# One core, hashed attention and two MLPs: hash matmuls in column halves, copies moved between engines, and a first head without on-chip DMAs

## The chip, the cores and the metric

The kernel runs on one core of a Trainium2 chip. The metric is the device time of one execution in microseconds (us). The kernel before takes 844.27 us (median of three runs, 843.8 to 844.47).

## The reference

Attention with a mask from a locality-sensitive hash, over 2 batches x 8 heads, 768 positions, 64 features a head, followed by two MLPs over all 1536 tokens (512 features, 2048 hidden), everything in float32:

```
q_bits = (q @ proj > 0); k_bits = (k @ proj > 0)        # proj: 64 x 6
mask   = bucket(q_bits) == bucket(k_bits)               # bucket: the 6 bits as a number
scores = where(mask, q @ k.T / 8, -1e9)
attn   = softmax(scores);  x = attn @ v                 # per head, then heads side by side
x = softplus(x @ w_in) @ w_out                          # first MLP
out = (h * clip(h + 3, 0, 6) / 6) @ w2_out, h = x @ w2_in
```

The weights of the MLPs arrive as 64-bit floats and are converted on the chip with integer operations.

## The kernel before, in words

**Precision.** Products run in a fast float32 form of TensorE (fp32r) on a high and a low part: `qa` holds the scaled q's high part in partitions 64 to 127 and its low part in 0 to 63, `ka` holds k's high part twice, `kb` k's low part in its first 64 partitions. The score of a tile is a matmul of `qa` with `ka` plus one of `qb` with `kb` (L392, L393); `qb` holds the high part of q, and the 32 rows from 64 on in `qb` and `kb` carry the hash bits, so that a pair of equal buckets gets a score apart from all others.

**A head.** `prepare(h)` loads k and q into one tile `raw` (k in partitions 0 to 63, q in 64 to 127), k twice into `rawk`, and v into `vx`. It makes the parts (L313 to L331), copies q's high part into `qb` by a DMA, and hashes: two float32 matmuls with 128 output columns (L340) accumulate the dots of both sequence halves in one PSUM tile `dots` of 128 rows (32 rows each for q and k of either half), one VectorE operation compares them (L356), and four DMAs bring the bits to the rows of `qb` and `kb` where they belong (L365). `attend(h)` goes through six tiles of 128 queries. Each has four score matmuls, the row maximum on VectorE (L406), a small bias operation (L413), the exponential on ScalarE (L421), six transposes on TensorE into one PSUM tile (L432), and a copy of these to SBUF (`even`; L226 is the copy helper on ScalarE, L228 on VectorE). When all six are there, the value matmuls run (L448), two at once, as each has 64 output columns and its own half of the PSUM rows. Then `xa` copies the result, three transposes turn it back (L470), `rec` is the reciprocal of the row sums (L474, L478) and `norm` multiplies by it (L485). For each pair of heads the normed result is transposed again (L512) and cut into high and low part: the first MLP's input.

**The MLPs.** For each of 2 layers, 3 groups of 512 tokens and 16 pieces of 128 hidden features: 12 hidden matmuls (L605), an activation chain over ScalarE, VectorE and (first layer only) one GpSimd subtraction (L231), and 12 matmuls into four accumulators (L697, L699). The weights are converted piece by piece (L552 to L576). Twelve of the first layer's 32 pieces are converted during the attention, the rest when SBUF comes free behind it, and the second layer's when the first layer's have been used.

**The order of the work.** All operations go into a `Schedule`: each with a cost per engine that may do it (A ScalarE, D VectorE, P GpSimd, T TensorE, S SyncE for DMA issues), what it reads and writes, and a due time (`prio`, from `TH`, `WHEN`, `STEP`, `PROJECT`, `ACTIVATE`, `AHEAD`). `run()` simulates the engines when the kernel is built: it takes, of the operations that can start soonest on an engine, the one with the lowest due time, and emits it. So each engine's order is fixed at build time by these numbers, and where an operation has costs for two engines, the simulation chooses the engine. On the chip each engine works its list in order and waits by semaphores. Score tiles have two PSUM buffers (`two0`, `two1`), transposes one (`two2`), `av` one, and hash, `pt` and `xt` share one (`pre`).

Of the kernel before, what the change touches and what calls it, by code (L numbers as in the profile page):

```python
# [34 lines left out]
TH = 11.573  # L35
WHEN = dict(load_p=-28.21, load_k=-19.20, load_q=-23.34, load_v=-10.79, high_k=-6.00, high_q=-5.57, low_k=-0.24, low_q=-7.00, copy_q=-8.00, dots=-16.00, bits=-14.00, send=-7.00, scores=-3.50, max=-5.62, exp=2.50, turn=0.70, even=4.80, values=17.62, back=16.00, rec=14.00, norm=21.73, x=21.98, x_high=18.00, x_low=15.78)
# [3 lines left out]
SAME = dict(A=0.13, D=0.13, P=0.1, T=0.0, S=0.0, H=0.0)  # L40
ISSUE, LATENCY, DONE = 0.625, 0.65, 0.74
LANES = 8
TICK, WARM = 3.413, 0.374
STEP = 5.682
PROJECT = 8.694
ACTIVATE = -18.000
FETCH = -52.296
AHEAD = 25.891


def f32(ap):
    return ap.bitcast(F32)
# [11 lines left out]
class Operation:  # L64
    def __init__(self, cost, emit, new, touched, prio, dma, duty):
        self.duty = duty
        self.cost, self.emit, self.new, self.touched, self.prio = cost, emit, new, touched, prio
        self.dma = dma
        self.deps, self.next, self.open = [], [], 0
        self.engine = self.done = None  # L70


class Schedule:
# [8 lines left out]
    def add(self, cost, emit, reads=(), writes=(), prio=0.0, after=(), uses=(), dma=0.0, duty=1.0):  # L82
# [3 lines left out]
        op = Operation(cost, emit, list(writes), {*reads, *writes, *uses}, prio, dma, duty)  # L86
# [11 lines left out]
    def run(self):  # L98
        free = dict(A=1.96, D=0.1, P=0.6, T=0.1, S=0.65, H=0.0, G=0.0, M=0.0)
        lanes, busy = [0.0] * LANES, {}  # L100
        ready = {op: self.times(op) for op in self.ops if not op.open}
        while ready:
            options = []
            for op, times in ready.items():
                slot = self.slots(op)
                if slot is not None:
                    for e, t in times.items():
                        at, end, unit = max(free[e], slot, t), op.cost[e], e
                        if e == "T" and busy.get(int(at / TICK) - 1, 0.0) < WARM * TICK:
                            end *= 2  # L110
# [12 lines left out]
            if e == "T":  # L123
                tick = int(start / TICK)
                busy[tick] = busy.get(tick, 0.0) + op.cost[e] * op.duty
# [46 lines left out]
def lsh_attention_two_mlps(  # L172
# [88 lines left out]
    for s0 in (0, D):  # L261
        plan.add(
            dict(S=0.625), lambda e, s0=s0: nc.sync.dma_start(out=p32.ap[s0 : s0 + D, :], in_=proj),
            writes=[p32], prio=WHEN["load_p"], dma=0.06,
        )
    hashes = buffer("heads", [P, 6 * ROWS], F32, "hash", 1, "hash")

    def set_hashes(e):
        nc.vector.memset(hashes.ap, 0.0)
        for i, sign in enumerate((1.0, -1.0)):  # L270
            for rows, c, s in ((slice(0, D), 3 * ROWS + NB * i, -sign), (slice(D, P), 2 * ROWS + NB * i, sign)):
                nc.vector.tensor_scalar(hashes.ap[rows, c : c + NB], p32.ap[rows, :], s, None, op0=ALU.mult)

    plan.add(dict(D=0.7), set_hashes, reads=[p32], writes=[hashes], prio=-20)
# [4 lines left out]
    def prepare(h):  # L279
# [4 lines left out]
        rawk = buffer("heads", [P, S], F32, "rawk", 2, f"rawk{h}")  # L284
        for d, n in ((qa, "qa"), (qb, "qb"), (ka, "ka"), (kb, "kb")):
# [12 lines left out]
        plan.add(  # L298
            first, lambda e: engines[e].dma_start(out=rawk.ap, in_=kv[head][:, :S]),
            writes=[rawk], prio=at + WHEN["load_q"], dma=1.1,  # L300
        )
# [6 lines left out]
        wide, narrow = dict(A=0.74, D=0.48), dict(D=0.88)  # L308

        def scaled(e):  # L310
# [8 lines left out]
            narrow,  # L319
# [5 lines left out]
        plan.add(  # L325
            wide, lambda e: cast(e, ka[h].ap, rawk.ap),
            reads=[rawk], writes=[ka[h]], prio=at + WHEN["high_k"],
        )
# [4 lines left out]
        plan.add(  # L333
            queue, lambda e: engines[e].dma_start(out=f32(qb[h].ap[0:D, :]), in_=f32(qa[h].ap[D:P, :])),
            reads=[qa[h]], writes=[qb[h]], prio=at + WHEN["copy_q"], dma=0.55,
        )
        dots = buffer("ps", [P, 512], F32, "pre", 1, f"d{h}")

        def dot(u):
            nc.tensor.matmul(  # L340
                dots.ap[:, :HALF], hashes.ap[:, (1 - u) * 2 * ROWS : (3 - u) * 2 * ROWS],
                raw.ap[:, u * HALF : (u + 1) * HALF], start=(u == 0), stop=(u == 1),
            )

        last = ()
        for u in range(2):
            last = [
                plan.add(
# [476 lines left out]
```

## Time and profile before

One execution was profiled. It took 844.39 us; the span of its instructions is 842.7 us, the other 1.7 us lie around it.

| | busy us | share of the span | instructions |
|---|---|---|---|
| TensorE matmul (PE) | 799.3 | 95% | 3808 |
| TensorE weight load (PEld) | 604.5 | 72% | 3808 |
| VectorE (DVE) | 558.9 | 66% | 958 |
| ScalarE (ACT) | 451.5 | 54% | 764 |
| GpSimd (POOL) | 92.1 | 11% | 85 |

The granted TensorE clock is full in nearly the whole span (0.999 on average). The load of k twice (`rawk`) moves 384 KB a head, those of k, q, v and the copy of q's high part 192 KB each. The attention takes the first 281 us, the first MLP the time to 573, the second the rest. Matmuls are pipelined and overlap in the records, so a TensorE that is shown busy need not be at its peak; the shares are averages over stages with different limits.

### The profile page before, as it was taken

The numbers are of one execution on the slowest core, as the hardware profiler recorded it, in microseconds if no ns is written. First come the engines' busy times: TensorE is split into PE (matmuls) and PEld (weight loads), VectorE is DVE, ScalarE is ACT, GpSimd is POOL, SyncE is SP. The second block draws the span as 40 slices with busy tenths as digits, with TensorE's granted clock in tenths as the row PEclk, the third lists the DMA queues.
The fourth block names the chain that finished last, engine by engine and source line by source line (L and its number), as shares of the span: only waits on it lengthen the run. The fifth ranks groups of instructions, "written<-read, shape, count | busy, mean of one in ns | idle before, by whom it ended". The sixth has DMA issues, their size and how long they took to land.

```text
span 842.7 us, 10395 instructions
## 1 busy us (share of the span) xinstructions
PE 799.3 (95%) x3808; PEld 604.5 (72%) x3808; DVE 558.9 (66%) x958; ACT 451.5 (54%) x764; POOL 92.1 (11%) x85
## 2 busy tenths in 40 slices
PE   4899999999999999999999999999999999999997
PEld 2666666666666667677888776677888888888886
DVE  4989999999887889964333698989942322232222
ACT  1677677777665767656554766775532322232222
POOL 1000000000000242322222224340000000000000
PEclk9999999999999999999999999999999999999999
DMA  7584323332310650000000255451000100010001
GB/s 191 166 271 103 82 80 93 86 85 75 86 29 28 254 228 0 1 1 1 0 1 1 93 157 167 158 175 50 1 1 1 50 1 1 0 51 1 1 0 51
DMA packets 26771, 59.40 MB, mean 70 GB/s; under 512 B 3680, under 2 KB 7776, under 8 KB 26720
## 3 DMA queue, kind: packets, MB, share of 16 engines
q1 hardware_dynamic: 24224, 52.45, 20.6%
q10 hardware_dynamic: 2496, 6.29, 2.1%
q8 instruction: 30, 0.49, 0.2%
q14 instruction: 21, 0.17, 0.1%
HBM read 49.29 MB, written 3.15 MB: 62 GB/s over the span
## 4 chain that ended last, share of the span: by engine, by line
PE 65%; DVE 16%; ACT 5%; DMA 5%; POOL 4%; issue 4%; SPq 1%; ACTq 0%; DVEq 0%; POOLq 0%
PE ph L605 22%; PE acc L699 16%; PE acc L697 7%; PE av L448 7%; PE tp L432 5%; POOL ml L231 4%; PE sc L392 4%; PE sc L393 3%; DVE gl L231 2%; DVE bits L576 2%; DVE bits L569 2%; PE d L340 2%; ACT e L421 2%; DMA raw<-in_moe_w_out_dram 2%; DVE me L665 2%
## 5 line engine op out<-in xcount | busy, mean ns | idle before, releaser
L605 PE MATMUL ph<-xh,w 128*128 128x512 f32 x768 | 240.8, 395 | 0.8 <-ACT xa L226 0.6
L605 PEld LDWEIGHTS ph<-xh,w 128*128 128x128 f32 x768 | 143.7, 188 | 34.5 <-ACT xa L226 1.3
L605 PE MATMUL ph<-xl,w 128*128 128x512 f32 x384 | 151.2, 394 | 0.0
L421 ACT ACTIVATE e<-sc,bs 128x768 f32<-128x768 f32 x96 | 95.0, 990 | 64.2 <-DVE bs L413 44.9
L634 DVE SCALAR_TENSOR_TENSOR ml<-me,ph 128x512 f32<-128x512 f32 x48 | 33.0, 687 | 124.6 <-ACT me L629 124.6
L697 PE MATMUL acc<-gh,w 128*128 128x512 f32 x384 | 101.0, 400 | 11.7 <-ACT gh L226 11.3
L231 POOL TENSOR_TENSOR ml<-ml,me 128x512 f32<-128x512 f32 x48 | 85.9, 1789 | 210.3 <-DVE me L665 154.2
L406 DVE TENSOR_REDUCE nm<-sc 128x1 f32<-128x768 f32 x96 | 91.7, 955 | 22.1 <-PE sc L393 20.6
L629 ACT ACTIVATE me<-ph,three 128x512 f32<-128x512 f32 x48 | 33.1, 689 | 133.7 <-PE ph L605 130.7
L699 PE MATMUL acc<-w,gh 128*128 128x512 f32 x384 | 97.8, 393 | 0.0
L697 PEld LDWEIGHTS acc<-gh,w 128*128 128x128 f32 x384 | 69.9, 188 | 37.2 <-ACT gh L226 22.7
L605 PEld LDWEIGHTS ph<-xl,w 128*128 128x128 f32 x384 | 72.1, 188 | 17.0
L699 PEld LDWEIGHTS acc<-w,gh 128*128 128x128 f32 x384 | 72.1, 188 | 16.7
L392 PE MATMUL sc<-ka,qa 128*128 128x384 f32 x192 | 76.7, 400 | 7.0 <-ACT e L421 6.6
L432 PE MATMUL tp<-ident,e 128*128 128x128 f32 x576 | 80.1, 275 | 3.2 <-DVE et L228 1.7
L432 PEld LDWEIGHTS tp<-ident,e 128*128 128x128 f32 x576 | 66.8, 140 | 16.0 <-ACT et L226 5.2
L448 PE MATMUL av<-et,vx 128*64 128x384 f32 x384 | 72.1, 498 | 0.0
L393 PE MATMUL sc<-kb,qb 96*128 96x384 f32 x192 | 66.1, 344 | 2.3 <-DMA kb<-bt 2.3
L392 PEld LDWEIGHTS sc<-ka,qa 128*128 128x128 f32 x192 | 36.8, 192 | 38.6 <-ACT e L421 15.5
L676 DVE SCALAR_TENSOR_TENSOR ml<-ph,ml 128x512 f32<-128x512 f32 x48 | 33.0, 687 | 38.7 <-POOL ml L231 38.7
L697 PE MATMUL acc<-gl,w 128*128 128x512 f32 x192 | 54.4, 397 | 2.8 <-ACT xh L226 2.1
L231 DVE TENSOR_TENSOR gl<-ml,gh 128x512 fp32r<-128x512 f32 x48 | 38.5, 801 | 26.0 <-ACT gh L226 26.0
(62 smaller groups left out, 1030.4 us busy)
## 6 DMA issues: line engine op xcount, KB each, us to landing
raw<-in_moe_w_in_dram SPq DMA_DIRECT2D x26, 512.0 KB, 4.6
raw<-in_moe_w_out_dram SPq DMA_DIRECT2D x26, 512.0 KB, 3.5
rawk<-in_kv_dram SPq DMA_DIRECT2D x16, 384.0 KB, 4.2
raw<-in_kv_dram SPq DMA_DIRECT2D x16, 192.0 KB, 3.2
raw<-in_q_dram SPq DMA_DIRECT2D x16, 192.0 KB, 3.4
vx<-in_kv_dram SPq DMA_DIRECT2D x16, 192.0 KB, 2.4
qb<-qa SPq DMA_DIRECT2D x16, 192.0 KB, 4.1
raw<-in_moe_w_in_dram ACTq DMA_DIRECT2D x6, 512.0 KB, 8.8
```

The costliest lines, as they stand in the source:

```text
L231: engines[e].tensor_tensor(out, a, b, op=ALU.subtract)
L392: nc.tensor.matmul(o, qa[h].ap[:, qs], ka[h].ap[:, cs], start=True, stop=False)
L393: nc.tensor.matmul(o, qb[h].ap[0:KB, qs], kb[h].ap[0:KB, cs], start=False, stop=True)
L406: lambda e, sc=sc, t=t: nc.vector.reduce_max(nm.ap[:, t, 0:1], sc.ap[:, :, :HALF], axis=AX.XY, negate=True),
L421: lambda e, sc=sc, ex=ex, t=t: nc.scalar.activation(ex.ap.rearrange("p (u k) -> p u k", u=2), sc.ap[:, :, :HALF], AF.Exp, bias=bs.ap[:, t, ...
L432: nc.tensor.transpose(o, ex.ap[:, c * P : (c + 1) * P], ident.ap)
L448: nc.tensor.matmul(av.ap[u * D : (u + 1) * D, :HALF], vx[h].ap[:, c, :], et[u].ap[:, c, :], start=(c == 0), stop=(c == NT - 1),)
L605: nc.tensor.matmul(bank(), w[:, a, :], x[b].ap[:, kc, :], start=(kc + i == 0), stop=(kc == KC - 1 and i == 2))
L629: dict(A=0.478), lambda e: nc.scalar.activation(e1.ap, bank(), AF.Relu, bias=three.ap),
L634: lambda e: nc.vector.scalar_tensor_tensor(l.ap, e1.ap, 6.0, bank(), op0=ALU.min, op1=ALU.mult),
L697: nc.tensor.matmul(o, w.ap[:, a, cs], b.ap, start=st, stop=sp)
L699: nc.tensor.matmul(o, b.ap[:, cs], w.ap[:, a, :], start=st, stop=sp)
```

## The change

The hash tile `hashes` shrinks from 192 to 64 columns, and its two matmuls write to the two halves of the PSUM rows, each with 64 output columns. They are one operation now. ScalarE alone does the scaling of q, the cast of k and the copy `xa` (except parts of head 0), and of the six `even` copies of a head the tiles 1, 2, 4 and 5; tiles 0 and 3 stay open to VectorE. GpSimd does the subtraction for k's low part (except head 0) and the small sum in `rec`. Head 0 loads no `rawk`, and gets `ka`, the copy of q's high part and the hash bits by compute engines: two half casts, one copy, and four VectorE operations of 32 rows. One of the two loads of `proj` is issued by ScalarE. The planner counts 0.09 where TensorE changes between three kinds of matmul, and all costs and due times get new values.

```diff
-TH = 11.573
+TH = 9.867
-STEP = 5.682
-PROJECT = 8.694
-ACTIVATE = -18.000
-FETCH = -52.296
-AHEAD = 25.891
+SWITCH = 0.09
+STEP = 5.895
+PROJECT = 9.269
+ACTIVATE = -18.456
+FETCH = -54.515
+AHEAD = 31.626
 ...
+                        if e == "T" and op.mode != mode:
+                            end += SWITCH
 ...
-    for s0 in (0, D):
+    for s0, e in ((0, "S"), (D, "A")):
-    hashes = buffer("heads", [P, 6 * ROWS], F32, "hash", 1, "hash")
+    hashes = buffer("heads", [P, 2 * ROWS], F32, "hash", 1, "hash")
 ...
+        if h:
+            rawk = buffer("heads", [P, S], F32, "rawk", 2, f"rawk{h}")
 ...
-        wide, narrow = dict(A=0.74, D=0.48), dict(D=0.88)
+        wide, narrow = dict(A=0.74) if h else dict(A=0.74, D=0.48), dict(P=1.9) if h else dict(D=0.88)
 ...
+            for s0, e in ((0, "D"), (D, "A")):
+                plan.add(
+                    {e: wide[e]}, lambda e, s0=s0: cast(e, ka[h].ap[s0 : s0 + D, :], raw.ap[0:D, :]),
+                    reads=[raw], writes=[ka[h]], prio=at + WHEN["high_k"] - s0,
+                )
 ...
+            plan.add(
+                dict(A=0.74), lambda e: cast(e, qb[h].ap[0:D, :], f32(qa[h].ap[D:P, :])),
+                reads=[qa[h]], writes=[qb[h]], prio=at + WHEN["high_q"],
+            )
 ...
-        def dot(u):
-            nc.tensor.matmul(
-                dots.ap[:, :HALF], hashes.ap[:, (1 - u) * 2 * ROWS : (3 - u) * 2 * ROWS],
-                raw.ap[:, u * HALF : (u + 1) * HALF], start=(u == 0), stop=(u == 1),
-            )
+        def dot(e):
+            for u in range(2):
+                nc.tensor.matmul(
+                    dots.ap[u * D : (u + 1) * D, :HALF], hashes.ap, raw.ap[:, u * HALF : (u + 1) * HALF],
+                    start=True, stop=True,
+                )
+        if h == 0:
+            for u in range(2):
+                for n, x in enumerate((qb, kb)):
+                    rows = slice((2 * u + n) * ROWS, (2 * u + n + 1) * ROWS)
+                    plan.add(
+                        dict(D=0.5),
+                        lambda e, u=u, x=x, rows=rows: nc.vector.tensor_scalar(
+                            x[h].ap[D:KB, u * HALF : (u + 1) * HALF], dots.ap[rows, :HALF], thr.ap[rows, 0:1],
+                            top.ap[rows, 0:1], op0=ALU.is_gt, op1=ALU.mult,
+                        ),
+                        reads=[dots, thr, top], writes=[x[h]], prio=at + WHEN["bits"],
+                    )
+            return
 ...
-                dict(A=0.81, D=0.95), even, reads=[tp], writes=[et[t // n]], prio=step + WHEN["even"],
+                dict(A=0.73) if t % 3 else dict(A=0.73, D=0.88), even, reads=[tp], writes=[et[t // n]], prio=step + WHEN["even"],
 ...
-            dict(A=0.49, D=0.46), lambda e: cast(e, xa.ap, av.ap[:, :HALF]),
+            dict(A=0.44), lambda e: cast(e, xa.ap, av.ap[:, :HALF]),
 ...
-            dict(D=0.08), lambda e: nc.vector.tensor_scalar(rec.ap, den.ap, 1e-9, None, op0=ALU.add),
+            dict(P=0.3), lambda e: nc.gpsimd.tensor_scalar(rec.ap, den.ap, 1e-9, None, op0=ALU.add),
 ...
-            dict(P=1.3), lambda e: minus(e, l.ap, l.ap, e1.ap), reads=[l, e1], writes=[l], prio=prio
+            dict(P=1.8), lambda e: minus(e, l.ap, l.ap, e1.ap), reads=[l, e1], writes=[l], prio=prio
```

## Rows read from the trace of the kernel before

**Rows 1.** Busy time by stretch: stretch, its us, each engine's busy us (instructions), granted clock.
```profile
35.10:260.20 225.10, 217.28 (x1308) 149.30 (x1307) 205.28 (x379) 158.07 (x273) 3.62 (x13) 1.00 0.37 104
281.20:363.80 82.60, 76.69 (x318) 57.56 (x318) 76.02 (x129) 56.89 (x100) 27.88 (x13) 1.00 0.24 90
```

**Rows 2.** Chain of waits, 115 to 132 us: start us, us, engine, tile, line.
```profile
115.67 0.68 PE d L340 x2
...
116.70 0.66 PE tp L432 x6
117.36 0.18 PE sc L392
...
117.71 0.65 PE d L340 x2
...
119.13 1.44 PE av L448 x8
120.57 0.37 PE sc L392
...
122.14 1.44 PE av L448 x8
...
128.15 0.34 PE pt L470 x3
...
129.76 0.96 DVE nm L406
```

**Rows 3.** Groups of instructions, 35.1 to 260.2 us: count, busy us, mean ns, idle before.
```profile
L421 ACT ACTIVATE e<-sc,bs 128x768 f32<-128x768 f32 x85 | 84.2, 990 | 45.8 <-DVE bs L413 39.2 <-DVE qa L320 3.2 <-DVE rec L478 1.6
...
L228 DVE COPY et<-tp 128x768 f32<-128x768 f32 x40 | 37.8, 946 | 0.4 <-PE tp L432 0.4
L226 ACT ACTIVATE et<-tp 128x768 f32<-128x768 f32 x44 | 35.6, 810 | 14.0 <-PE tp L432 13.3
...
L231 DVE TENSOR_TENSOR kb<-raw,ka 64x768 fp32r<-64x768 f32 x13 | 12.2, 942 | 0.0
...
L228 DVE COPY xa<-av 128x384 f32<-128x384 f32 x10 | 5.6, 558 | 2.4 <-PE av L448 2.0
```

**Rows 4.** Instructions in order of time, 0 to 36 us.
```profile
0.80 1.23 SPq L263 DMA_DIRECT2D p<-in_proj_dram  x2
...
2.85 0.16 DVE L272 TENSOR_SCALAR hash<-p 64x6 f32<-64x6 f32 x1 [1.73 <-DMA p<-in_proj_dram]
...
3.21 0.60 SPq L295 DMA_DIRECT2D raw<-in_q_dram  x1
...
7.74 2.90 PE L340 MATMUL d<-raw,hash 128*128 128x384 f32 x4 [7.74 <-DMA raw<-in_q_dram]
...
10.75 0.68 DVE L356 TENSOR_SCALAR bt<-d,thr,top 128x384 fp32r<-128x384 f32 x1 [0.60 <-PE d L340]
...
12.64 0.58 SPq L365 DMA_DIRECT2D kb<-bt  x1
...
17.90 0.66 PE L393 MATMUL sc<-kb,qb 96*128 96x384 f32 x1 [2.33 <-DMA kb<-bt]
```

**Rows 5.** GpSimd's and VectorE's instructions in order of time, in the first MLP.
```profile
309.68 1.62 POOL L231 TENSOR_TENSOR ml<-ml,me 128x512 f32<-128x512 f32 x1 [3.34 <-DVE me L665]
310.06 1.53 DVE L557 TENSOR_SCALAR bits<-bits 128x512 f32<-128x512 f32 x1
311.51 0.75 DVE L562 TENSOR_SCALAR bits<-bits 128x512 int32<-128x512 int32 x2
...
371.64 1.29 POOL L231 TENSOR_TENSOR ml<-ml,me 128x512 f32<-128x512 f32 x1 [3.87 <-DVE me L665]
```

**Rows 6.** Waits: 40 to 260, 281 to 573, 363.8 to 472 us; us, times, longest.
```profile
ACT et L226 <- PE tp L432: 13.3, 17, 1.6
...
DVE ml L676 <- POOL ml L231: 38.7, 29, 1.5
...
DVE ml L676 <- POOL ml L231: 24.9, 17, 1.5
```

More of the change, by code (lines that the diff above doesn't have):

```diff
@@ L64, with __init__ @@
 class Operation:
-    def __init__(self, cost, emit, new, touched, prio, dma, duty):
-        self.duty = duty
+    def __init__(self, cost, emit, new, touched, prio, dma, mode):
+        self.mode = mode
         self.cost, self.emit, self.new, self.touched, self.prio = cost, emit, new, touched, prio
@@ L80, in __init__, with add @@
         self.ops, self.rings = [], {}
-    def add(self, cost, emit, reads=(), writes=(), prio=0.0, after=(), uses=(), dma=0.0, duty=1.0):
+    def add(self, cost, emit, reads=(), writes=(), prio=0.0, after=(), uses=(), dma=0.0, mode="r"):
         deps = list(after)
@@ L85, in add @@
             deps += b.users if b in writes else b.writers
-        op = Operation(cost, emit, list(writes), {*reads, *writes, *uses}, prio, dma, duty)
+        op = Operation(cost, emit, list(writes), {*reads, *writes, *uses}, prio, dma, mode)
         for b in op.touched:
@@ L124, in run @@
                 tick = int(start / TICK)
-                busy[tick] = busy.get(tick, 0.0) + op.cost[e] * op.duty
+                busy[tick] = busy.get(tick, 0.0) + op.cost[e]
+                mode = op.mode
             free[e] = op.done
@@ L324, in prepare @@
         )
[L325 to L328, printed above, removed]
+        if h:
+            plan.add(
+                wide, lambda e: cast(e, ka[h].ap, rawk.ap),
+                reads=[rawk], writes=[ka[h]], prio=at + WHEN["high_k"],
+            )
+        else:
+            for s0, e in ((0, "D"), (D, "A")):
[3 more added lines that the diff above has]
+                )
         plan.add(
@@ L345, in prepare @@
[L345 to L348, printed above, removed]
-                    dict(T=0.66), lambda e, u=u: dot(u),
-                    reads=[raw, hashes], writes=[dots], prio=at + WHEN["dots"], after=last,
-                )
-            ]
+        if h:
+            plan.add(
+                queue, lambda e: engines[e].dma_start(out=f32(qb[h].ap[0:D, :]), in_=f32(qa[h].ap[D:P, :])),
+                reads=[qa[h]], writes=[qb[h]], prio=at + WHEN["copy_q"], dma=0.55,
+            )
+        else:
+            plan.add(
+                dict(A=0.74), lambda e: cast(e, qb[h].ap[0:D, :], f32(qa[h].ap[D:P, :])),
+                reads=[qa[h]], writes=[qb[h]], prio=at + WHEN["high_q"],
+            )
@@ L432, in turn @@
                     nc.tensor.transpose(o, ex.ap[:, c * P : (c + 1) * P], ident.ap)
-            plan.add(dict(T=0.56), turn, reads=[ex, ident], writes=[tp], prio=step + WHEN["turn"])
+            plan.add(dict(T=0.5), turn, mode="t", reads=[ex, ident], writes=[tp], prio=step + WHEN["turn"])
             def even(e, tp=tp, t=t):
```

40 lines of the change are left out of this document (18 added, 22 removed).

## The prediction

> **What bounds the kernel now.** I read the table of stretches first, then the chain of waits, then the groups of instructions, then the first 36 us in order of time. The stretch with 14 of the 16 heads, from the first exponential of head 1 to that of head 15, is 225.1 us long [rows 1], and holds 84 exponentials, six a head, and one more at its edge [rows 3]. So a head takes 225.1 / 14 = 16.08 us. TensorE is busy for 97% of it, VectorE for 91%, ScalarE for 70% (217.28, 205.28 and 158.07 of 225.1), at the upper clock level (2.4 GHz, granted 1.00). Two engines that high leave open which one limits, and a busy TensorE need not be at its peak; the chain answers that. Through the head at 115 us it runs along TensorE instruction behind instruction for some 13 us, and leaves it only at the end of the head, where VectorE's max, copy and subtraction stand in it [rows 2].
>
> TensorE's own need per head can be added up from that chain [rows 2]. A tile with values goes from one av group to the next: 122.14 - 119.13 = 3.01 us, three times: 9.03. A tile without them is six transposes at 0.66 and four score matmuls at 0.18: 1.38, three times: 4.14. The hash is two pieces, 0.68 and 0.65: 1.33. The turn back of the head (pt) is 0.34, and of the x transposes (six per two heads) half of a 0.66 falls to a head: 0.33. Sum 15.2 us. The other 16.08 - 15.2 = 0.9 us is waiting for another engine, mostly at the head's end. So TensorE is the bound, VectorE close behind.
>
> Behind the attention the two MLP layers run at TensorE's pace except where weights are converted: from 281.2 to 363.8 us VectorE is busy for 76.02 of 82.6 us and TensorE issues 318 matmuls [rows 1]; there VectorE limits.
>
> **The change part by part.**
>
> Hash in column halves. Now it is two matmuls with 128 output columns, 1.33 us a head [rows 2]. Afterwards it is two with 64, which can stream together, as the av matmuls do (128x64 against 384 columns). Their eight records take 1.44 us, so four take 0.72. The av group shows two prices beside that: eight records at twice the rate of the hash pieces (0.34 a record) would be 8 x 0.17 = 1.36, so 0.08 is spent at its ends, and the first score matmul behind it takes 0.37 instead of 0.18 [rows 2]. So 0.72 + 0.08 + 0.19 = 0.99, a gain of 0.34; without these prices it is 1.33 / 2 = 0.67. I take 0.45 per head, as the hash may also stand next to an av group and share its switch.
> The Trainium skill, TensorEngine Tiling (Array Packing), section Key Properties, says that a change of tiling mode drains the engine; the 0.37 against 0.18 agrees with it. The section Theoretical Speedup promises up to 2x; by that alone a head would gain 0.67, and the attention 3 us more.
>
> Work taken off VectorE, per head, from [rows 3], divided by 14 heads. The low part of k goes to GpSimd: 0.94. Copies of the transposed tiles: 40 / 14 = 2.86 are on VectorE now, at most 2 (every third of six tiles) may be afterwards: 0.86 x 0.95 = 0.81. The xa copy, 10 of 14: 0.40. The scaled q, the k cast and the small sum for the reciprocal, each now on VectorE in some heads: 0.45 together, an estimate from the same rows by their size. Sum 2.6: VectorE falls from 205.28 / 14 = 14.7 to 12.1 us a head. ScalarE gets these copies at its own price (0.81 for a transposed tile, the others in proportion): 0.70 + 0.35 + 0.3 + 0.1 = 1.5, and rises from 158.07 / 14 = 11.3 to 12.8. Both then stand below TensorE's 15.2 - 0.45 = 14.75. So none of this counts directly; it counts only in the 0.9 us of waits. Least: nothing goes (the wait at the head's end is a chain through several engines, and ScalarE is now late in it). Most: all 0.9. I take 0.55, nearer to all than to none, since VectorE's ops stand in that gap in the chain and VectorE then has 2.6 us more room.
>
> GpSimd's subtraction. No row shows 64x768 there. 128x512 takes 1.29 us undisturbed [rows 5], so 768 columns 1.29 x 1.5 = 1.93 us, in front of which nothing is queued but small fills and, new, the sum for the reciprocal. k is ready most of a head early, so 1.93 instead of 0.94 is hidden. What isn't free: GpSimd and VectorE stood in each other's way in the MLP. Beside a subtraction there a 128x512 tensor_scalar took 1.53 us, where two of its kind together take 0.75, and the subtraction itself 1.62 [rows 5]. Bounds per head: nothing (if only max, bias and copies from PSUM fall beside it), or one hindered op, 1.53 - 0.38 = 1.15, stretched by 1.5 to 1.7 of VectorE's time. VectorE has that room, so I take nothing for TensorE.
>
> Attention together: 0.45 + 0.55 = 1.0 us a head over heads 1 to 15: -15 us. Bounds: 0.67 + 0.9 = 1.57 a head gives -24; nothing gained gives 0; a loss is the last rival.
>
> The first head. Now its first finished scores start at 17.90 us, behind this chain [rows 4]: q is issued at 3.21, behind p twice, rawk (the doubled k) and k, and is seen at 7.74; the hash takes 2.90 (four records at twice the 0.34 of later ones), the bits 0.68 from 10.75, then the DMA of the bits is issued at 12.64 and seen 5.3 us later. Afterwards k and q are SP's first DMAs, from 0.80 on, and no rawk is loaded. A tiny DMA is seen 2.85 - 0.80 = 2.05 us after its issue; q with rawk and k, 768 KB, 4.53. So 192 KB cost (4.53 - 2.05) / 4 = 0.6, and q, issued second, at about 1.4, is there at 1.4 + 2.05 + 2 x 0.6 = 4.7, and p, third on SP and on the ACT queue, by about the same. Then VectorE has the hash weights, four at 0.16; half of the k cast, 0.6 at most (by the bits); two low parts at 0.95; four bit ops of 32 rows at 0.6, as columns and not rows set their time: 5.5 us, to 10.2 [rows 3, 4]. ScalarE's three copies at 0.81 and the hash (half of 2.90) lie beside it. So scores start at 10.2 instead of 17.90: -7.7. Bounds: -5.5 (p late by 2) to -8.5. Three kinds of DMA waits go from head 0; those of head 1 are issued earlier and have the whole of head 0 as cover.
>
> The MLP. Its instructions stay; GpSimd's planned cost (1.3 to 1.8) and the due times change the order. VectorE's wait for GpSimd's subtraction is 38.7 us in 281 to 573, of which 24.9 lie in the stretch where TensorE is full and cost nothing [rows 6]. The other 13.8 are what a better order could win at most; a worse one could cost as much. The same instructions, so I take 0.
>
> Sum against the profiled run, 844.39 us (span 842.7 and 1.7 around it; the median of the runs is 0.12 less): 844.3 - 15 - 7.7 = 821.6, or 822 us.
>
> **The rivals.**
>
> *All waits go, and the MLP's order gets better*: 844.3 - 24 - 7.7 - 7 (half of the 13.8) = 806. For it: VectorE gets 2.6 us of room a head. Against it: six tiles pass through two score buffers and one transpose buffer as before.
>
> *ScalarE takes VectorE's place.* Its copies of transposed tiles waited 13.3 us in 17 waits for the transposes, 0.78 each [rows 6]. With four a head, 3.1 us of wait on 12.8 of work make 15.9 against the 16.08 of now, 0.18 a head. Beside that the first head's gain stays: 844.3 - 7.7 - 15 x 0.18 = 834. Against it: a wait in which the engine has nothing due costs nothing.
>
> *The halves don't run at once*: the hash takes 1.33 + 0.27 of switching instead of 1.33 - 0.45 = 0.88; 16 x 0.72 = 11.5 us are missing: 833. Against it: av shows such pairs together.
>
> *GpSimd gets between VectorE and TensorE*, at the head's end. The sum for the reciprocal now stands on GpSimd behind the subtraction, and behind that the reciprocal, xn and the x transposes. If the subtraction starts just before it, it is 1.93 us late, and TensorE has nothing else to do there; a hindered bias op in front of an exponential would cost the same. At 1.93 a head 822 + 15 x 1.93 = 851. It decides from 22.3 / 15 = 1.5 us a head on. For it: the waits at the head's end are there already [rows 2]. Against it: the subtraction is due long before.
> The Trainium skill, SBUF — State Buffer, section Who interferes with whom, says that a VectorE op with two SBUF inputs and a GpSimd op that reads SBUF exclude each other for a whole instruction; the 1.53 us agree for a neighbouring kind, and no run here shows it yet for the bias op, which by that rule would be hit.
>
> **How the numbers follow.** The forecast, 822, has 0.55; all waits gone 0.18; ScalarE 0.13; halves in turn 0.06; GpSimd 0.06; 0.02 for a change that ends within what can be told from none (0.2%, 1.7 us). The range goes from the second case to past the third and fourth: 806 to 836. Faster: all but the last two and part of the ScalarE case, 0.91; same 0.03; slower 0.06.
>
> **What would show it.** Four hash records a head in about 0.8 us with the first score behind them at 0.37. Finished scores from 10 to 11 us. Head to head 15.1 us, TensorE nearer to 15 of that, VectorE near 12, ScalarE near 13. GpSimd's 64x768 at 1.9 us or more. From the last value matmul to the end 561 us (842.7 - 281.2), as now. Wrong if the heads still take 16 us with another engine in the gaps, or the MLP moves by more than 5 us.

## The result and the profile after

The changed kernel takes 832.48 us (median; 832.43 to 832.95) against 844.03 us of the kernel before, run beside it: a ratio of 0.9866, with a 95% interval of 0.9848 to 0.9883. The forecast was 822 us in a range of 806 to 836. So the sign was right and the time lies in the range, but the gain is 11.6 us where 22 had been forecast.

The table of stretches of the changed kernel, to be read beside [rows 1]: stretch, its us, busy us (instructions) of TensorE's matmuls, its weight loads, VectorE, ScalarE and GpSimd, then the granted clock, the DMA share and GB/s. The first stretch goes from the first exponential of head 1 to that of head 15, the second is heads 2 to 5, the third heads 6 to 14; the others are short stretches that are read further down.

```profile
27.60:246.90 219.30, 211.17 (x1305) 143.48 (x1303) 170.75 (x308) 183.91 (x314) 30.05 (x40) 0.99 0.38 109
46.00:110.40 64.40, 59.60 (x367) 40.41 (x366) 62.97 (x119) 59.45 (x103) 9.30 (x12) 1.00 0.45 127
110.40:246.90 136.50, 134.67 (x844) 91.46 (x842) 92.96 (x164) 110.69 (x189) 17.61 (x25) 1.00 0.28 77
...
22.00:26.00 4.00, 2.95 (x20) 2.35 (x19) 3.78 (x5) 2.82 (x5) 1.92 (x2) 1.00 0.20 47
26.00:30.00 4.00, 3.29 (x12) 3.20 (x13) 2.69 (x6) 2.77 (x6) 0.67 (x1) 0.59 0.82 226
265.00:270.00 5.00, 3.89 (x18) 2.88 (x16) 4.62 (x7) 4.36 (x9) 1.35 (x1) 1.00 0.94 366
270.00:275.00 5.00, 3.70 (x12) 2.82 (x13) 5.00 (x9) 4.49 (x9) 1.77 (x2) 0.75 0.03 11
```

The same view of the kernel before, cut at the same heads (2 to 5, then 6 to 14):

```profile
50.40:114.90 64.50, 61.67 (x371) 41.99 (x370) 59.17 (x109) 45.37 (x78) 0.84 (x4) 1.00 0.42 112
114.90:260.20 145.30, 140.82 (x850) 97.00 (x849) 131.96 (x243) 100.65 (x174) 2.68 (x8) 1.00 0.28 73
```

The reader is to see that the relief of VectorE is real (170.75 instead of 205.28 us in heads 1 to 14) and that the gain is not spread evenly. Heads 6 to 14 went from 145.30 / 9 = 16.14 us to 136.50 / 9 = 15.17 us, and TensorE is now busy in 134.67 of the 136.50. Heads 2 to 5 take 64.40 / 4 = 16.10 us, as before, with TensorE idle for 4.8 us. Heads 1 to 14 together went from 225.10 [rows 1] to 219.30 us, 0.41 us a head. TensorE's idle time in them has not fallen: 225.10 - 217.28 = 7.8 us before, 219.30 - 211.17 = 8.1 us now.

Divided at the starts of the exponentials, the 12.1 us by which the span is shorter (842.7 to 830.6) come from these places. (In this table heads 2 to 5 and 6 to 14 are means per head.)

| us | before | after | change in all |
|---|---|---|---|
| first exponential of head 0 at | 20.49 | 13.15 | -7.3 |
| head 0 | 14.6 | 14.4 | -0.2 |
| head 1 | 15.2 | 18.4 | +3.1 |
| heads 2 to 5, each | 16.13 | 16.12 | 0 |
| heads 6 to 14, each | 16.14 | 15.17 | -8.8 |
| head 15 to the first hidden matmul | 13.3 | 12.2 | -1.1 |
| first hidden matmul to the end | 569.2 | 571.5 | +2.3 |

A single head says little: the cut leaves 87 to 101 of TensorE's matmul records in each of heads 6 to 14 of the changed kernel, and these heads take 14.3 to 16.2 us.

What divides heads 2 to 5 from the later ones is shown by the last integer operation of each early weight conversion. The groups of instructions of the changed kernel, 50 to 115 us (count, busy us, mean ns):

```profile
L603 DVE SCALAR_TENSOR_TENSOR bits<-raw,bits 128x512 int32<-128x512 int32 x11 | 7.4, 674 | 0.0
```

The same of the kernel before, 115 to 180 us:

```profile
L576 DVE SCALAR_TENSOR_TENSOR bits<-raw,bits 128x512 int32<-128x512 int32 x5 | 3.3, 683 | 0.0
```

Before, the twelve pieces were spread over heads 1 to 13, the last one ending at 235.8 us: by this operation three of them stood in heads 2 to 5 and eight in heads 6 to 14. Now the planner puts ten into heads 2 to 5, and the last one reaches into head 6 and ends at 115.6 us. Behind that no head holds a conversion. So the two groups are not the same work before and after: heads 6 to 14 lost seven of their eight pieces, and heads 2 to 5 took on seven. Only heads 1 to 14 together hold the same twelve in both kernels.

The chain of waits of the changed kernel, in a head that holds none (start us, us, engine, tile, line), to be read beside [rows 2]:

```profile
118.68 0.66 PE tp L459 x6
119.34 0.17 PE sc L419
...
120.04 1.44 PE av L475 x8
121.48 0.82 PE tp L459 x6
...
123.03 1.09 ACT e L448 x2
...
125.13 0.71 PE tp L459 x6
125.84 0.80 PE d L361 x4
126.64 0.38 PE sc L419
```

The hash is four records in 0.80 us where it was 0.68 and 0.65, and the first score behind it takes 0.38.

The groups of instructions of the changed kernel, 27.6 to 246.9 us, beside [rows 3]:

```profile
L448 ACT ACTIVATE e<-sc,bs 128x768 f32<-128x768 f32 x84 | 83.2, 990 | 19.5 <-DVE bs L440 13.5 <-DVE rec L505 3.9 <-PE tp L459 1.2
L231 ACT ACTIVATE et<-tp 128x768 f32<-128x768 f32 x70 | 56.6, 808 | 13.8 <-PE tp L459 13.1
L236 POOL TENSOR_TENSOR kb<-raw,ka 64x768 fp32r<-64x768 f32 x13 | 23.7, 1822 | 64.3 <-ACT ka L231 63.7 <-DMA kb<-bt 0.3 <-PE av L475 0.2
...
L233 DVE COPY et<-tp 128x768 f32<-128x768 f32 x14 | 13.3, 948 | 2.2 <-PE tp L459 2.2
```

VectorE makes one copy of transposed tiles a head (14 in 14 heads) where it made 2.86, and GpSimd's subtraction takes 1.82 us.

The first instructions of the changed kernel in order of time (start us, us, engine, line, operation, tiles, shapes, and in brackets the idle time before it and what ended it), beside [rows 4]:

```profile
0.78 0.59 SPq L295 DMA_DIRECT2D raw<-in_kv_dram  x1
...
1.43 0.57 SPq L299 DMA_DIRECT2D raw<-in_q_dram  x1
...
4.79 0.56 DVE L321 TENSOR_SCALAR qa<-raw 64x768 fp32r<-64x768 f32 x1 [0.31 <-DMA raw<-in_q_dram]
...
6.13 1.55 PE L361 MATMUL d<-raw,hash 128*64 128x384 f32 x4 [6.13 <-DVE hash L277]
...
8.08 0.67 DVE L373 TENSOR_SCALAR qb<-d,thr,top 32x384 fp32r<-32x384 f32 x1
...
9.72 0.69 PE L420 MATMUL sc<-kb,qb 96*128 96x384 f32 x1 [1.42 <-ACT qb L231]
...
10.93 0.69 PE L420 MATMUL sc<-kb,qb 96*128 96x384 f32 x1 [0.21 <-DVE kb L373]
```

### The profile page after: what moved, and what is told of

Read it like the earlier page. It is cut to its first block, busy times and chain, and to the rows that moved or that the text cites. A ratio compares the mean times of both kernels' runs of the same rounds, so it can differ in the third digit from the quotient of the medians.

```text
span 830.6 us, 10443 instructions
## 1 busy us (share of the span) xinstructions
PE 793.9 (96%) x3808; PEld 596.3 (72%) x3808; DVE 519.8 (63%) x878; ACT 484.7 (58%) x818; POOL 117.6 (14%) x116
## 4 chain that ended last, share of the span: by engine, by line
PE 69%; DVE 18%; ACT 5%; issue 4%; POOL 2%; DMA 1%; POOLq 0%; SPq 0%; ACTq 0%; DVEq 0%
PE ph L632 22%; PE acc L726 16%; PE acc L724 7%; PE av L475 7%; PE tp L459 6%; PE sc L419 4%; PE sc L420 3%; DVE bits L603 3%; DVE w L236 2%; POOL ml L236 2%; DVE bits L596 2%; DVE gl L236 2%; DVE bits L589 2%; DVE bits L584 1%; DVE nm L433 1%
## 5 line engine op out<-in xcount | busy, mean ns | idle before, releaser
L724 PE MATMUL acc<-gh,w 128*128 128x512 f32 x384 | 103.9, 409 | 9.2 <-ACT gh L231 8.9
L236 POOL TENSOR_TENSOR ml<-ml,me 128x512 f32<-128x512 f32 x48 | 80.4, 1676 | 218.7 <-DVE me L692 142.3
L459 PE MATMUL tp<-ident,e 128*128 128x128 f32 x576 | 82.2, 279 | 1.8 <-ACT et L231 1.0
L231 ACT ACTIVATE et<-tp 128x768 f32<-128x768 f32 x79 | 63.9, 808 | 15.1 <-PE tp L459 14.2
L236 DVE TENSOR_TENSOR gl<-ml,gh 128x512 fp32r<-128x512 f32 x48 | 36.8, 767 | 35.7 <-ACT gh L231 35.7
L679 ACT ACTIVATE me<-ph 128x512 f32<-128x512 f32 x48 | 28.4, 591 | 48.2 <-PE ph L632 48.1
```

Source lines behind the costliest of these rows:

```text
L231: nc.scalar.activation(out, in_, AF.Copy)
L236: engines[e].tensor_tensor(out, a, b, op=ALU.subtract)
L459: nc.tensor.transpose(o, ex.ap[:, c * P : (c + 1) * P], ident.ap)
L724: nc.tensor.matmul(o, w.ap[:, a, cs], b.ap, start=st, stop=sp)
```

## The experiments

Ratios are to the kernel before, run beside each kernel on the same chip; the changed kernel's is 0.9866. Where a difference between two variants is given in us, it is the difference of their ratios times 844. "Order kept" means that every engine's list of instructions is that of the kernel named (the changed one, or the one before), and only what one entry does is another.

**Hash at full width again, order kept.** The hash tile has 192 columns again.

```diff
-    dots.ap[u * D : (u + 1) * D, :HALF], hashes.ap, raw.ap[:, u * HALF : (u + 1) * HALF],
-    start=True, stop=True,
+    dots.ap[:, :HALF], hashes.ap[:, (1 - u) * 2 * ROWS : (3 - u) * 2 * ROWS],
+    raw.ap[:, u * HALF : (u + 1) * HALF], start=(u == 0), stop=(u == 1),
```

> The changed kernel with its order of work kept to the letter, but each head's hash again as two matmuls with 128 output columns that accumulate. In the changed kernel's trace a hash holds TensorE for 0.80 us, in the one before for 1.39 us, so 15 heads lose up to 9 us. First theory (TensorE's own work sets the pace of a head, and the column halves are where the heads' gain comes from): slower than the changed kernel by 5 to 9 us, 837 to 841 us. Rival (the heads gain because VectorE was relieved, and TensorE has room for the longer hash): within 2 us of 832.5. Rival of the forecast (the switch into column halves takes back 0.2 to 0.3 us a head): 836 us or less.

Measured: 837.36 us, ratio 0.9913 (0.99 to 0.9926), 4.0 us more than with halves. Heads 6 to 14 take 15.43 us instead of 15.17, heads 2 to 5 16.36 instead of 16.12. So the halves are worth 0.25 us a head here, about half of the 0.45 of the forecast. (The first exponential starts at 14.2 us instead of 13.1, which is part of the 4.0.)

The table of stretches of this experiment, heads 1 to 14, and its chain of waits at a hash with the same neighbours as the one shown above at 125.84:

```profile
29.50:251.80 222.30, 214.18 (x1303) 148.63 (x1301) 171.41 (x308) 183.56 (x314) 30.07 (x40) 1.00 0.38 107
...
127.65 0.70 PE tp L459 x6
128.35 1.29 PE d L361 x4
129.65 0.17 PE sc L419
```

Heads 1 to 14 take 222.30 us here, 15.88 a head. That is 0.20 less than in the kernel before: so much comes from all the rest of the change. The halves bring the other 0.21 of the 0.41.

**The hash in halves alone, in the kernel before, order kept.** The two matmuls of the change replace those at L340, at the place of the second.

> The kernel before with its order kept, and only the hash in column halves (both matmuls where the second stood). First theory (a head loses what the hash loses on TensorE, 1.39 to 0.80 us, less some switching): faster than the kernel before by 4 to 8 us, 836 to 840 us. Rival (VectorE is the bound of the kernel before, so TensorE's saving vanishes): within 2 us of 844.3.

Measured: 843.73 us, ratio 0.9989 (0.9979 to 0.9998). Heads 2 to 5 take 16.17 us and heads 6 to 14 16.06, against 16.13 and 16.14. The records are as short as in the changed kernel (median 537 ns, two at a time), so the halves run at once here too. The table of stretches, heads 1 to 14:

```profile
35.00:259.40 224.40, 213.76 (x1308) 142.87 (x1307) 205.07 (x379) 158.23 (x272) 3.62 (x13) 1.00 0.36 104
```

TensorE is busy for 3.5 us less than the 217.28 of the kernel before, and idle for 10.6 us instead of 7.8: most of what the hash saves turns into waiting. The gain of 0.9 us in all is all that is left, with VectorE as full as it was.

**The low part of k subtracted by VectorE again, order kept.**

```diff
-    narrow, lambda e: minus(e, kb[h].ap[0:D, :], ...
+    narrow, lambda e: minus("D", kb[h].ap[0:D, :], ...
```

> The changed kernel with the planned order kept, but the subtraction for k's low part is issued on VectorE instead of GpSimd (0.94 us a head of VectorE's time against 1.82 on GpSimd). In the changed kernel's trace 6 of 15 such subtractions shut out a small bias operation, which takes up to 1.82 us instead of 0.15, and 2 shut out a weight conversion: 8.7 us in sum. First theory (GpSimd's subtraction holds up the chain from the maximum to the exponential, and so takes back most of what VectorE's relief gives): faster than the changed kernel by 3 to 7 us, 826 to 830 us. Rival (VectorE's room is worth more than these stops): slower by 3 us or more, 836 us up. Third (neither matters, since TensorE has its work): within 1.5 us of 832.5.

Measured: 833.16 us, ratio 0.9866 (0.9851 to 0.9881): the same as the changed kernel. Heads 6 to 14 take 15.29 us. With the copies gone from VectorE, it does not matter which of the two engines subtracts; heads 2 to 5 take 16.14 us too. Whether it mattered with them was not tried.

**The bias operation with one input at a time.** It is the 128x2 operation with two SBUF inputs that stands in front of each exponential; here it is two operations of 128x1.

```diff
-    lambda e, t=t: nc.vector.scalar_tensor_tensor(
-        bs.ap[:, t, :], nm.ap[:, t, 0:1].to_broadcast([P, 2]), 0.5 * BIG, nm.ap[:, t, :], ...
+    lambda e, t=t: (
+        nc.vector.tensor_scalar(bs.ap[:, t, 1:2], nm.ap[:, t, 0:1], 0.5 * BIG, None, op0=ALU.is_lt),
+        nc.vector.tensor_scalar(bs.ap[:, t, 0:1], nm.ap[:, t, 0:1], 0.5 * BIG, nm.ap[:, t, 0:1], ...),
+    ),
```

> The changed kernel with the planned order kept; the small bias operation of a tile (one VectorE operation with two SBUF inputs) is made of two operations with one SBUF input each. GpSimd keeps the subtraction. If an operation with two SBUF inputs is what GpSimd shuts out, the stops of 0.4 to 1.8 us in front of exponentials go, at the price of 96 more short VectorE operations (about 0.07 to 0.1 us each, in the chain to the exponential). First theory: 2 to 5 us faster than the changed kernel, 827 to 830 us, and no bias operation above 0.3 us in the trace. Rival (the stop comes with any operation that reads SBUF, or the price of the second operation eats the gain): 832 us or more.

VectorE and GpSimd of the changed kernel, in order of time, around one subtraction:

```profile
167.00 1.82 DVE L440 SCALAR_TENSOR_TENSOR bs<-nm 128x2 f32<-128x2 f32 x1
168.85 0.95 DVE L326 SCALAR_TENSOR_TENSOR qa<-raw,qa 64x768 fp32r<-64x768 f32 x1
...
166.97 1.83 POOL L236 TENSOR_TENSOR kb<-raw,ka 64x768 fp32r<-64x768 f32 x1 [12.59 <-ACT ka L231]
```

The same place of this experiment:

```profile
168.36 0.15 DVE L441 TENSOR_SCALAR bs<-nm 128x1 f32<-128x1 f32 x1
168.44 0.20 DVE L442 TENSOR_SCALAR bs<-nm 128x1 f32<-128x1 f32 x1
169.22 1.88 DVE L326 SCALAR_TENSOR_TENSOR qa<-raw,qa 64x768 fp32r<-64x768 f32 x1 [0.58 <-ACT qa L319]
...
168.45 1.82 POOL L236 TENSOR_TENSOR kb<-raw,ka 64x768 fp32r<-64x768 f32 x1 [12.69 <-ACT ka L231]
```

In the changed kernel the bias operation starts with the subtraction and is held until it ends: 1.82 us, where it takes 0.15 undisturbed. In the experiment it passes, and the next operation with two SBUF inputs is held instead (1.88 us, where it takes 0.95). Measured: 832.65 us, ratio 0.9856 (0.9841 to 0.9871): not told apart from the changed kernel. So GpSimd does shut VectorE out, 6 of the 96 bias operations are hit (0.41 to 1.82 us), and it costs nothing that can be measured. Heads 2 to 5 take 16.18 us.

**Head 0 with its DMAs, as the other heads.** The order is planned anew.

```diff
-        if h:
+        if True:      # rawk, ka from rawk, qb's high part by DMA
-        if h == 0:
+        if False:     # the four bit operations
```

> The changed kernel with head 0 made as in the kernel before: k loaded twice, high part of q and hash bits moved by DMAs. The order is planned anew. First theory (a later start of head 0 is passed on in full): slower by 6 to 8 us, 838 to 841 us, finished scores near 17 us instead of 9.7. Rival (the early heads wait for their loads and weight conversions anyway, so a late start is made up): within 2 us of 832.5.

Measured: 840.93 us, ratio 0.9952 (0.994 to 0.9965), 7.3 us more than the changed kernel. The first exponential starts at 20.2 us instead of 13.1. So the first head is most of the whole gain.

**VectorE may take all copies again.**

```diff
-    dict(A=0.73) if t % 3 else dict(A=0.73, D=0.88), even, ...
+    dict(A=0.73, D=0.88), even, ...
-    dict(A=0.44), lambda e: cast(e, xa.ap, av.ap[:, :HALF]),
+    dict(A=0.44, D=0.46), lambda e: cast(e, xa.ap, av.ap[:, :HALF]),
-    wide, narrow = dict(A=0.74) if h else dict(A=0.74, D=0.48), ...
+    wide, narrow = dict(A=0.74, D=0.48), ...
```

> The changed kernel, in which VectorE may again take all copies that it might take before: every transposed tile, the scaled q, the cast of k, xa. GpSimd keeps its subtraction; the order is planned anew. First theory (copies matter only where VectorE is the bound, which is heads 1 to 5): slower by 1 to 4 us, 833.5 to 836.5 us. Rival of the forecast (the copies' move gives half of the waits, 0.55 us a head): slower by 8 us, 840 us. Third (they matter nowhere): within 1 us of 832.5.

The table of stretches of this experiment, heads 1 to 14:

```profile
27.30:259.70 232.40, 214.38 (x1305) 143.38 (x1304) 218.45 (x371) 143.53 (x251) 29.91 (x40) 0.99 0.35 102
```

and its groups of instructions in that stretch:

```profile
L233 DVE COPY et<-tp 128x768 f32<-128x768 f32 x63 | 59.9, 950 | 8.3 <-PE tp L459 8.2
...
L231 ACT ACTIVATE et<-tp 128x768 f32<-128x768 f32 x21 | 17.0, 809 | 6.7 <-PE tp L459 6.4
```

Measured: 846.56 us, ratio 1.0016 (1.0001 to 1.003): the gain is gone. Left free, and with the new due times, the planner gives VectorE 63 of 84 copies (40 before the change), and VectorE is busy for 94% of a stretch that is 13 us longer. The heads 6 to 14 take 16.33 us. I had expected the freedom to cost little; that theory fell, and no theory on record went as far.

**The new numbers alone, in the kernel before.** `TH`, `WHEN`, `STEP`, `PROJECT`, `ACTIVATE`, `FETCH` and `AHEAD` are the changed kernel's, and nothing else.

> The kernel before with nothing changed but the due times (TH, WHEN, STEP, PROJECT, ACTIVATE, FETCH, AHEAD), which are those of the changed kernel; costs, engines and instructions stay. First theory (the new due times fit the new split of work only, and by themselves change little): within 3 us of 844.3. Rival (the new due times are themselves what shortens the heads): 838 us or less. Third (they cost by themselves, and the structure's parts make up for it): 847 us or more.

Measured: 854.05 us, ratio 1.0102 (1.0087 to 1.0116). VectorE makes 58 of 84 copies of transposed tiles, heads 2 to 5 take 17.22 us, and first hidden matmul to end 576.7 us (the early conversions reach into that part here, so it doesn't price the MLP's due times by itself). The new numbers are worth nothing alone. What the new structure takes with the old numbers was not tried.

**The early conversions spread again.** In the first form the load of early piece n waits for head n's last exponential.

```diff
-    convert_all(0, range(EARLY), [first_exp])
+    for n in range(4 * EARLY):
+        j, i = divmod(n, 4)
+        prio = time_of(0, 0, 2 * j + max(0, i - 2)) - AHEAD
+        convert(0, j, i, (prio - FETCH, prio), [exps[n]])
```

> The changed kernel, in which each of the twelve early weight pieces may be loaded only when one more head has had its last exponential (piece n behind head n). In the changed kernel's trace the twelve conversions end at 115 us, where they ended at 235 us before; heads 1 to 5 take 16.6 us each with VectorE busy for 15 to 16 of them, heads 6 to 14 take 15.2 with VectorE at 10. First theory (with VectorE's room the planner packs the conversions into heads 1 to 5, makes VectorE the bound there and leaves its room unused later): faster by 4 to 7 us, 826 to 829 us, with heads 1 to 5 near 15.5 us. Rival (the early heads are slow because of their DMAs or the GpSimd subtraction, whatever VectorE does): within 1.5 us of 832.5, with heads 1 to 5 still above 16.3.

Measured: 837.85 us, ratio 0.9913 (0.9891 to 0.9935), 4.0 us slower than packed. Heads 2 to 5 take 15.96 us, heads 6 to 14 15.68. I had expected the packing to be what costs; that fell. But ScalarE waited 2.4 us for the weights' DMAs there, so a second form loads early and lets only the conversion of piece n wait, for the last exponential of head n + 1 (`convert(0, j, i, (prio - FETCH, prio), [exps[0]], [exps[n + 1]])`, where the last argument holds its first operation).

> The changed kernel; the twelve early weight pieces are loaded as before, behind head 0, but the conversion of piece n may start only behind the last exponential of head n + 1. The order is planned anew. First theory (packed conversions cost heads 1 to 5 about 1 us each, and the later heads have 4 to 5 us of VectorE free): 2 to 5 us faster than the changed kernel, 827.5 to 830.5 us. Rival (TensorE pauses more often with VectorE's long operations among the later heads, as in the kernel where the loads were spread, 837.9 us): 833 us or more.

The table of stretches of the second form, heads 2 to 5 and 6 to 14:

```profile
42.80:106.50 63.70, 59.97 (x374) 40.56 (x370) 52.65 (x93) 52.65 (x90) 8.64 (x12) 1.00 0.44 121
106.50:249.80 143.30, 136.34 (x845) 91.66 (x843) 116.40 (x210) 115.60 (x198) 17.53 (x25) 1.00 0.27 73
```

Measured: 836.51 us, ratio 0.9892 (0.9876 to 0.9908). Heads 2 to 5 take 63.70 / 4 = 15.92 us with one conversion each, heads 6 to 14 143.30 / 9 = 15.92 too. With two and more conversions a head the changed kernel had 16.10. So, on average, heads that hold conversions take about 16 us whether they hold one or more, heads without one 15.2 (heads 6 to 14 of the changed kernel), and of the three orders tried packing is the cheapest. The DMAs of the weights are not what lengthens them: in the second form all twelve pieces have landed by 55.8 us, the DMA share in heads 6 to 14 is 0.27 where the changed kernel has 0.28, and the heads still take 15.92.

**What it is in a conversion: VectorE's load?** The four integer operations of VectorE are left out for the twelve early pieces, order kept; these weights are not converted.

```diff
+    skip = layer == 0 and j < EARLY
-    lambda e: nc.vector.tensor_scalar(f32(b.ap), f32(b.ap), EXP_MIN, EXP_MAX, ...
+    lambda e: skip or nc.vector.tensor_scalar(f32(b.ap), f32(b.ap), EXP_MIN, EXP_MAX, ...
```

(and so for the other three)

> The changed kernel with its order kept; left out are the four VectorE integer operations of each of the twelve early weight pieces (2.2 us of VectorE a piece, 26 us in all, nearly all in heads 1 to 5). Output: the first MLP's early weights are not converted. First theory (VectorE bounds heads 1 to 5 of the changed kernel, because the early conversions are packed there): heads 2 to 5 fall from 16.1 to about 15.1 us, and the whole to 826 to 829 us. Rival (they wait for something else, such as DMAs, the GpSimd subtraction, or the order in which ScalarE takes exponentials and copies): heads 2 to 5 stay above 15.7 and the whole above 831.

Measured: 830.1 us, ratio 0.9823 (0.9809 to 0.9837). In heads 2 to 5 VectorE is busy for 47.29 us of 63.60 instead of 62.97 of 64.40, and a head still takes 15.91 us. A quarter of VectorE's load taken away gives 0.2 us a head. The whole lies between the two theories, 826 to 829 and above 831.

**Or ScalarE's load?** The same with ScalarE's two operations of each early piece left out also, VectorE making two plain copies in their place.

```diff
-    lambda e: skip or nc.vector.tensor_scalar(f32(b.ap), f32(b.ap), EXP_MIN, ...
+    lambda e: cast("D", f32(b.ap), f32(high())) if skip else nc.vector.tensor_scalar(f32(b.ap), ...
-    lambda e: cast(e, both.ap[:, 0, :], f32(b.ap)), ...
+    lambda e: cast("D" if skip else e, both.ap[:, 0, :], f32(b.ap)), ...
```

> The changed kernel with its order kept; of each of the twelve early weight pieces both ScalarE operations (1.3 us a piece, 15 us in all) and VectorE's integer operations are left out; VectorE makes two plain copies in their place. Output: the first MLP's early weights are not converted. With VectorE's operations alone left out, heads 2 to 5 stayed at 15.8 to 16.0 us and ScalarE was busy for 14.3 to 15.4 of them. First theory (ScalarE, with its new copies and 2.5 early pieces a head, bounds heads 2 to 5): they fall to 14.5 to 15.3 us and the whole to 824 to 827 us. Rival (TensorE's pauses there come from the order of the copies and the exponentials, not from ScalarE's load): heads 2 to 5 stay above 15.6 us and the whole above 829.

The table of stretches of this experiment, heads 2 to 5:

```profile
46.40:110.10 63.70, 59.12 (x364) 40.14 (x364) 53.39 (x98) 49.86 (x84) 8.77 (x12) 1.00 0.46 128
```

and TensorE's waits in it (what waited, for what: us in total, times, longest):

```profile
PE sc L419 <- ACT e L448: 3.2, 4, 1.1
PE d L361 <- DVE xn L512: 0.9, 1, 0.9
```

TensorE's waits in the changed kernel, heads 2 to 5:

```profile
PE sc L419 <- ACT e L448: 2.4, 3, 1.1
PE d L361 <- DVE xn L512: 0.8, 1, 0.8
PE xt L539 <- DVE bt L383: 0.5, 1, 0.5
PE tp L459 <- ACT et L231: 0.5, 1, 0.5
```

Measured: 832.37 us, ratio 0.9845 (0.983 to 0.9859); heads 2 to 5 take 15.94 us. ScalarE has fallen from 59.45 to 49.86 us there, and the waits stand: one a head for an exponential, of up to 1.1 us. In heads 6 to 14 of the changed kernel that same wait adds up to 1.0 us in nine heads. ScalarE's load is now 12.5 us a head, and heads 6 to 14 of the changed kernel take 15.17 with 12.3 (110.69 / 9). So neither engine's load makes the 16 us. What these kernels have in common is the order of the instructions, written for heads with conversions in them. That the order is the cause is not shown directly: it is what is left when the loads of the two engines, the weights' DMAs, GpSimd's subtraction and the stop of the bias operation are excluded. Which neighbour delays the exponential was not isolated.

**The value matmuls of the last head before the second hidden piece.** The changed order puts 24 of them behind three hidden pieces, at 277 to 281 us, and the granted clock falls around 272 us behind a pause of TensorE.

```diff
+        if (layer, g, f) == (0, 0, 1):
+            last = [*last, *gate["values"]]
```

> The changed kernel, in which the second hidden piece of the first MLP must come behind the value matmuls of the last head. In the changed kernel's trace these values stand behind three hidden pieces, at 277 us; before that TensorE stops from 268.9 to 270.9 us, and then matmuls run at half pace (granted clock 0.75 from 270 to 275 us). First theory (the MLP's part of the shortfall, 2.9 us from the first hidden matmul on, is this stop and the lower clock behind it): 2 to 3.5 us faster than the changed kernel, 829 to 830.5 us, granted clock 1.00 there. Rival (the first MLP groups wait for weight conversions on VectorE anyway, so what is won at 270 us is lost by 360): within 1 us of 832.5.

The table of stretches of this experiment:

```profile
268.00:275.00 7.00, 4.23 (x21) 3.45 (x22) 7.00 (x12) 3.81 (x8) 1.09 (x1) 1.00 0.20 82
```

Measured: 834.76 us, ratio 0.988 (0.9861 to 0.9899), 1.2 us more than the changed kernel; the two intervals overlap, and neither theory had said it. The clock stays at its upper level (2.4 GHz, granted 1.00) and no gain can be seen: VectorE is busy for all of these 7.00 us, as it was for all of 270 to 275. From the first hidden matmul to the end it is 574.4 us.

## Why the forecast was right in sign and half in size

**The first head was right.** Forecast -7.7, measured -7.3 at the first exponential; undone alone it gives 7.3 back. Its steps are there: q is seen at 4.79 us (4.7 forecast), the finishing score matmuls start at 9.72 and 10.93 (10.2 forecast). The hash took 1.55 us, where half of 2.90 had been forecast, and started only when its weights were made, at 6.13.

**The failed step is the sum over the heads: "1.0 us a head over heads 1 to 15: -15 us".** Measured: -8.8 + 0 + 3.1 for heads 1 to 14 and -1.1 for head 15, that is -6.8. Over heads 1 to 14, which hold the same conversions in both kernels, it is 0.41 a head instead of 1.0, and both terms of the sum are too large. The hash, forecast at 0.45, gives 0.21 to 0.25 (full width again, order kept). All the rest, for which the forecast has 0.55 of the 0.9 us of waits, gives 0.20. The waits did not go: TensorE is idle for 8.1 us in these heads where it was for 7.8.

Where they stayed is shown by the tables. In heads 6 to 14 TensorE now waits for 1.8 us in all, 0.2 a head; in heads 2 to 5 it waits for 4.8, 1.2 a head, and there the forecast's own sign of being wrong has come, heads of 16 us. I had treated all heads as alike, since the order of before had spread the conversions. The planner used VectorE's new room to pack them into heads 1 to 5. The heads 6 to 14 won 0.97 each and stand at 15.17, where 15.1 was forecast, with TensorE busy for 99%; but this does not confirm the 1.0, since seven of eight conversions left these heads at the same time. With eight pieces in them again (second form of the spread order) they take 15.92, only 0.2 less than the 16.14 of before. In head 1 3.1 us were lost. It takes 16.1 us where the conversions begin in head 2 (second form), and 17.9 and 18.3 where they stay in their places and VectorE's or both engines' operations are left out; so there, too, it is more the places of the conversions than their load, and the cause was not isolated further. Packing was still the better of the orders tried (836.5 and 837.9 us with them spread).

That the time lies next to the 833 and 834 us of two rivals is chance: the halves run at once, and ScalarE's load is not what TensorE waits for.

**Why the hash's term came out at half.** Its own time is what was worked out, 0.80 us in four records with a first score of 0.38 behind. The 0.45 hoped that the hash would stand next to a group of value matmuls and share its switch. In heads 2 to 14 it never does: it stands between transposes and scores, and pays for its switch alone. At the place shown, with the same neighbours, the full-width hash takes 1.29 and the score behind it 0.17; in halves it is 0.80 and 0.38. The transposes in front take 0.70 and 0.71, so they are no part of it. The gain is 0.49 - 0.21 = 0.28 there. And with the rest of the kernel as before it is worth 0.9 us in all (0.9989). So the two terms of the forecast, 0.45 for the hash and 0.55 for the waits, don't add up independently: with VectorE at 91%, TensorE's shorter list mostly waited more.

**The copies were priced only by the waits that they leave.** VectorE fell to 170.75 / 14 = 12.2 us a head (12.1 forecast) and ScalarE rose to 183.91 / 14 = 13.1 (12.8 forecast). What I did not see is how much hangs on the copies being forbidden to VectorE: with the new due times and without the rule the kernel takes 846.56 us.

**ScalarE's load did not take VectorE's place.** Its copies waited 13.1 us for transposes [rows 6 had 13.3], and in heads 6 to 14 TensorE is at 99% all the same. In heads 2 to 5 TensorE's longest waits are for ScalarE's exponentials (2.4 us of 4.8), but they stay when ScalarE's load falls to 49.86 us.

**GpSimd did not get between VectorE and TensorE, though its mechanism is there.** The rule of the Trainium skill, SBUF — State Buffer, section Who interferes with whom, which was weighed in the forecast, holds for the bias operation: 1.82 us beside a subtraction. The price is what failed to come: 1.93 a head had been set for it, and neither taking the lock off the bias operation (832.65) nor the subtraction on VectorE (833.16) changes the time. The subtraction starts when k has been cast, once a head; that the operations it holds up have slack there is inferred from these two runs and not traced. Its duration, 1.82, was forecast at 1.93 from [rows 5].

**The MLP was forecast at 0 and lost 2.3 us.** From the first hidden matmul to the end it is 570.8 to 576.7 us in all kernels with the new numbers and 569.2 to 569.3 in the two with the old; that is within the bounds of 13.8 that the forecast gave. VectorE's waits for GpSimd's subtraction fell from 38.7 [rows 6] to 32.3 us in 275 to 573 without a gain. The fall of the clock is not the cause: it is absent from the kernel with the values put first, which takes 574.4, and from the one in which VectorE subtracts, which takes 570.8. Which of the new numbers it is, a due time or GpSimd's planned cost, stays open. The forecast's own marker, 561 us from the last value matmul, can't be read any more, since three hidden pieces now come before the last of those matmuls, where one did.

## What to carry to other kernels

A term "so much a head" holds only for heads with the same work in them: before multiplying, look which of them also carry work that the planner may move, and ask where it goes when an engine gets room. Afterwards, compare only stretches that hold the same work: a group of heads that comes out as forecast may have lost work to its neighbours. Shortening one of two engines that were both above 90% busy gave 0.7 us over heads 1 to 14 here, and 3.0 once the other was relieved; so price the pair. To part a duration from an order, keep every list as it is and change only what one entry does.

## What the runs showed of the hardware that was not expected

GpSimd's 64x768 subtraction holds even a 128x2 VectorE operation with two SBUF inputs for its whole length (1.82 us instead of 0.15), while 128x1 operations with one input beside it take 0.15 and 0.20.

Four records of 128x64 against 384 columns, two at once, take 0.80 us against 1.33 for the full-width pieces, and the score behind pays as well: 0.38 instead of 0.17 or 0.18. The transposes in front take the same (0.71 against 0.70 at the same place in the kernel with the full-width hash).

The changed kernel's granted clock falls towards the lower level (1.2 GHz, half of the upper) in two places where the kernel before keeps 1.00: it is 0.59 on average from 26 to 30 us and 0.75 from 270 to 275. Both lie behind stretches in which TensorE was busy only in part (2.95 of 4.00 us from 22 to 26, 3.89 of 5.00 from 265 to 270). That alone does not bring a fall: in the kernel with the full-width hash TensorE is busy for 2.39 of 4.00 us from 26 to 30, and the granted clock stays at 1.00 there and to 34 us. Neither fall can be seen in the time: without the first, in that same kernel, head 1 still takes 18.0 us, and without the second, with VectorE subtracting, the stretch from the first hidden matmul to the end takes 570.8 us instead of 571.5.
